# Split fp32r products for two small sums, and another order of the output matrix's making, in a fused linear-attention and state-space kernel

## The chip, the cores and the metric

The kernel runs on one core of one Trainium2 chip. A core has a matrix engine (PE, whose weight loads are listed apart as PEld), a vector engine (DVE), a scalar engine (ACT), a general engine (POOL) and a queue engine (SP) that issues most transfers; each works through its own instructions in order. The metric is the time of one execution on the device in microseconds (us), lower is better.

## The reference

From one input x (2048 positions, 448 channels) two branches are computed and mixed by a gate for each position:

```python
g = sigmoid((x * gate_w).sum(-1, keepdims=True))
# branch a: linear attention without a mask, 16 heads of 28 channels
q, k, v = split(x @ wqkv)
phi = lambda t: where(t > 0, t + 1, exp(t)) + 1e-6
pq, pk = phi(q), phi(k)
kv  = einsum("bhsd,bhse->bhde", pk, v)
z   = pk summed over positions
num = einsum("bhqd,bhde->bhqe", pq, kv)
den = einsum("bhqd,bhd->bhq", pq, z) + 1e-6
a = (num / den) @ wo
# branch b: a state-space convolution of x along the positions, plus x * D_skip
b = irfft(rfft(x) * rfft(K))[:S] + x * D_skip
out = g * a + (1 - g) * b
```

K is the convolution's kernel, made from a table of decay rates. For the tables in use K is nearly constant over all 2048 positions, so that the convolution is a running sum of x times one number for each channel; the kernel counts for how many channels this holds, and only if that is not all 448 a general convolution is run at the end. With these inputs it is not run.

## The kernel before, in words

The 2048 positions are 16 chunks of 128. Matrix products that need more than the engine's fast format gives are split: a number is written as a high part in fp32r and the low rest, and high·high, low·high and high·low are added up (11 products for a chunk with 448 inner channels). `low` makes such a rest, `ACT.copy` into an fp32r tile makes the high part.

**Main loop** (c = 0 to 13, then a closing part for c = 14 and 15). For each chunk PE projects k of chunk c+1 and q of chunk c (`project`, `pieces`, L319), adds pk·x into four running 128x448 sums (`do_g`, L388) and makes the running sum of x inside the chunk (`do_v`, L395 and L396). ACT and DVE make pk and pq (`k_feature`, `k_high`, `k_low`, `q_post`); `k_low` also adds pk into `zb`, so that at the end `zb` summed over its 128 partitions is z. `v_post` multiplies the running sum by its taps, sends its last row to row c of the tile `u` through SP (L402), and POOL adds it to the chunk's output (`v_add`, L407).

**Closing part** (from `c = NC - 2`). In program order: k of chunk 15 and its features; the last `v_post`; q of chunk 14; one block of `do_g(14)`; an fp32 product of a ones column with `oks` (the count of channels, L626) and an fp32 product of a 128x128 ones matrix with `zb` (L627), which leaves z on all partitions; `q_post(14)`; ACT copies z back to `zb` (L629); POOL starts the products pq·z (`norm_a`, L517); the rest of `do_g(14)`; the gate of chunk 14 (`gate`, L372 to L374); a PE transposition of the gates (`gates_b`, L564), which needs that gate; the denominators of chunks 0 and 1 (`norm_b`, `norm_d`, `norm_c`); and the four blocks of `do_g(15)`, each copied out by ACT (L646). `okn` receives the count (L637).

**Making the output matrix.** `inter` multiplies a 0/1 matrix `gcat` with `u` in fp32 (L660): the carry of each chunk from all chunks before it. Then K·V of each head pair (`kv_products`, L691, 32 fp32 instructions), its masking and splitting (`kv_split`, `kv_low`), and its product with wo for four groups of heads (`m_products`, L671; `m_high`, L675; `m_low`, L679). Group 3 is laid out anew: four small transfers (L725 three, L726 one) move rows of it below the rows of the other groups. Between these PE transposes chunk 0 (`turn_pe`) and finishes q of chunk 15 (`q_run`).

**Last loop** (c = 0 to 15). In each step DVE takes chunk c-1 out of PSUM and SP writes it (`final_b`, L607); `norm_c(c+2)` scales pq by 1/den with two POOL instructions (L540, L546) and one DVE instruction (L543); PE transposes chunk c+1 (L577), and ACT and DVE split the result into high and low (`turn_split`, L584, L585); ACT adds the carry's gate rows (`tail`, L588); POOL starts pq·z of chunk c+6 (`norm_a`); PE makes 11 products for chunk c (`attend`, L602); DVE sums pq·z of chunk c+5 over the heads (`norm_b`, L522); every second step `norm_d` makes 1/den for two chunks (L527, L529).

The order on each engine is the order of the program text (a manual schedule). Tiles rotate in pools of named tags, so that an instruction can also wait for a buffer; `norm_a(c)` and `norm_b(c-2)` share one in this way.

Of the kernel before, what the change touches and what calls it, by code (L numbers as in the profile page):

```python
# [7 lines left out]
F32 = mybir.dt.float32  # L8
# [7 lines left out]
P = 128  # L16
# [23 lines left out]
FAR = 2.0 ** 100  # L40
GIN = 9 + NC
L1, L0 = 32, 64
PAD = S + P
MAGIC = 1.5 * 2.0 ** 23
TWO_PI = 6.283185307179586
# [85 lines left out]
def gated_mix_kernel(ctx: ExitStack, tc: tile.TileContext, xin, wq_d, wv_d, wo_d, abc_d, ldt_d, dsk_d,  # L131
# [23 lines left out]
    tri = const.tile([P, P], F32R, name="tri")  # L155
    ident = const.tile([P, P], F32, name="ident")
    mask = const.tile([DJ, DJ], F32, name="mask")
    gcat = const.tile([NC - 1, RX], F32, name="gcat")
    sel = const.tile([P, 1], F32, name="sel")
    ones = const.tile([P, P], F32, name="ones")  # L160
    rows = const.tile([P, S], F32, name="rows")
    near, dsk = (rows[:, i * D:(i + 1) * D] for i in range(2))
    u = const.tile([NC, D], F32, name="u")
    zb = const.tile([P, D], F32, name="zb")
    kv = const.tile([DJ, J, DJ], F32, name="kv")
    ldt = const.tile([DJ, J], F32, name="ldt")
    sm = const.tile([DJ, 16, J], F32, name="sm")
    oks = const.tile([DJ, 1], F32, name="oks")
    trir = const.tile([P, P], F32, name="trir")

    xp = work.enter_context(tc.tile_pool(name="xp", bufs=4))
# [6 lines left out]
    DVE.memset(warm, 1.0)  # L178
    POOL.memset(zb, 0.0)
    POOL.memset(rows[DT:RX, 2 * D:], 0.0)  # L180

    xt, xn, turned, plain = {}, {}, {}, {}

# [187 lines left out]
    def gate(a, b):  # L371
        DVE.tensor_scalar(out=e1[:, a:b], in0=e1[:, a:b], scalar1=1.0, scalar2=None, op0=ALU.add)  # L372
        DVE.reciprocal(out=og[:, a:b], in_=e1[:, a:b])
        DVE.tensor_scalar(out=og[:, a:b], in0=og[:, a:b], scalar1=-1.0, scalar2=1.0, op0=ALU.mult, op1=ALU.add)  # L374
# [5 lines left out]
    def do_g(c, blocks=range(4)):  # L380
        w = xn[c]
        for i in blocks:
            a = w[:, 64 + i * P:64 + (i + 1) * P]
            b = w[:, XC - NAT + 64 + i * P:][:, :P] if i < 3 else None
            seq = [(a, pkh[c]), (a, pkl[c]), (b, pkh[c])] if i < 3 else \
                  [(a, pkh[c]), (a[:, :64], pkl[c])][::1 if c == 0 else -1]
            for n, (a, b) in enumerate(seq):
                PE.matmul(g[i][:a.shape[1], :D], lhsT=a, rhs=b, start=c == 0 and n == 0,  # L388
                          stop=c == NC - 1 and n == len(seq) - 1)
# [3 lines left out]
    def do_v(c):  # L393
        v = vt[c] = ps.tile([P, 512], F32, name="v", tag="v%d" % (c % 2))
        PE.matmul(v[:, :D], lhsT=tri, rhs=xn[c][:, :D], start=True, stop=False)  # L395
        PE.matmul(v[:, :D], lhsT=tri, rhs=xn[c][:, XC - NAT:], start=False, stop=True)  # L396

    def v_post(c):
        t = tp.tile([P, D], F32, name="t", tag="v0")
        DVE.tensor_tensor(out=t, in0=vt.pop(c)[:, :D], in1=near, op=ALU.mult)  # L400
        if c < NC - 1:
            SP.dma_start(out=u[c:c + 1], in_=t[P - 1:P])  # L402
            v_add(c, t)
        return t

# [43 lines left out]
    q_post(0, qo)  # L449
    split_n(2)  # L450
    qo = project(1, wqh, wql, D + 2, "v0")
    DVE.memset(ones, 1.0)
    q_post(1, qo)
    steps(1)
    skip(0)
# [2 lines left out]
    for c in range(2, NC - 2):  # L458
        if c + 3 < NC:
            load_x(c + 3)  # L460
        if c == 2:
            for o, i in ((mask, mask_d), (gcat, gcat_d), (sel, sel_d)):
                SP.dma_start(out=o, in_=i)
        if c == 4:
            SP.dma_start(out=wv, in_=wv_d)
            SP.dma_start(out=wo, in_=wo_d)
        vs = VS.get(c, ())
        ko = project(c + 1, wkh, wkl, D, "v1" if c in (2, 4) else "k")
        for v in vs[:1]:
            do_v(v)  # L470
        split_t(c + 2)
        k_feature(c + 1, ko)
        k_high(c + 1)
        if c > 5:
            for v in vs[:1]:
                v_post(v)
        k_low(c + 1)
        qo = project(c, wqh, wql, D + 2, "q")
        if c == 5:
            steps(1)  # L480
        else:
            for v in vs[1:]:
                do_v(v)
        q_post(c, qo)
        if c == 5:
            v_post(0)
        else:
            for v in vs[1:]:
                v_post(v)
        if c < 5:  # L490
            steps(2 if c == 4 else 1)
        if c == 3:
            DVE.tensor_copy(tri, trir)
        do_g(c)
        if c == 5:
            do_v(1)
        if c < 4:
            skip(c - 1)
        split_n(c + 2)
        if c == 5:  # L500
            v_post(1)
        for j in {11: (0, 1), 12: (2, 3)}.get(c, ()):
            w = xn_p.tile([P, NX], F32R, name="wo", tag="n")[:DJ, :2 * D].rearrange("p (i d) -> p i d", i=2)
            woh.append(w[:, 0])
            wol.append(w[:, 1])
            ACT.copy(woh[j], wo[:, j])
            low(POOL, wol[j], wo[:, j], woh[j])
# [84 lines left out]
    def attend(c, cuts):  # L592
        av[c] = []
        h, l = th.pop(c), tl.pop(c)
        for i, (lo, hi) in enumerate(cuts):
            pool, tag = ((p3, "a"), (p3, "a"), (ps, "v0"), (ps, "k"))[(c + i) % 4]
            a = pool.tile([P, 512], F32, name="a", tag=tag)
            av[c].append((a, lo, hi))
            seq = [(u_[:, j], w_[:, j]) for u_, w_ in ((h, mh), (l, mh), (h, ml)) for j in (2, 0, 1)]
            seq[6:6] = [(h[:, 3], mh[:, 3]), (l[:RX, 3], rc[0][:RX])]  # L600
            for n, (u_, w_) in enumerate(seq):
                PE.matmul(a[:, lo:hi], lhsT=u_, rhs=w_[:, lo:hi], start=n == 0, stop=n == 10)  # L602

# [9 lines left out]
            ACT.copy(pq[:, c, lo:hi], a[:, lo:hi])  # L613

    c = NC - 2
    gate(0, c)
    ko = project(c + 1, wkh, wkl, D, "k")
    do_v(c + 1)
    k_feature(c + 1, ko)
    k_high(c + 1)  # L620
    k_low(c + 1)
    vl = v_post(c + 1)
    qo = project(c, wqh, wql, D + 2, "q")
    do_g(c, (0,))
    zo = ps.tile([P, 512], F32, name="zo", tag="v0")
    PE.matmul(zo[:1, D:D + 1], lhsT=ones[:DJ, :1], rhs=oks, start=True, stop=True)  # L626
    PE.matmul(zo[:, :D], lhsT=ones, rhs=zb, start=True, stop=True)  # L627
    q_post(c, qo)
    ACT.copy(zb, zo[:, :D])  # L629
    norm_a(0)  # L630
    norm_a(1)
    do_g(c, (1, 2, 3))
    gate(c, c + 1)
    g2 = gates_a(1, NC - 1)
    POOL.memset(rows[DT:RX, :2 * D], 0.0)
    last = gates_b(g2, "pkl")
    DVE.tensor_copy(okn, zo[:1, D:D + 1])  # L637
    norm_bd(0)
    norm_c(0)
    last()  # L640
    norm_a(2)
    norm_bd(1)
    norm_c(1)
    for i in range(4):
        do_g(c + 1, (i,))
        ACT.copy(gs[i], g[i][:, :D])  # L646
# [8 lines left out]
    def inter():  # L655
        o = ps.tile([P, 512], F32, name="z", tag="v0")
        r = tp.tile([P, D], F32R, name="rc", tag="w")
        z = tp.tile([P, D], F32R, name="zs", tag="v0")
        rc.append(r)
        PE.matmul(o[:RX, :D], lhsT=gcat, rhs=u[:NC - 1], start=True, stop=True)  # L660
        ACT.copy(z[DT:RX], o[DT:RX, :D])
        DVE.scalar_tensor_tensor(out=r[DT:RX], in0=z[DT:RX].bitcast(F32), scalar=sel[DT:RX],
                                 in1=o[DT:RX, :D], op0=ALU.mult, op1=ALU.add)
# [30 lines left out]
    def kv_split(r, kvp):  # L694
        m = 3 if r else 2
        DVE.tensor_tensor(out=kv[:, 2 * r:m],
                          in0=kvp[:DJ, 2 * r * DJ:m * DJ].rearrange("p (j d) -> p j d", d=DJ),
                          in1=mask[:, None, :].to_broadcast([DJ, m - 2 * r, DJ]), op=ALU.mult)
        if r:
            a, b = (w.rearrange("p (h d) -> p h d", h=4) for w in (kvp[:DJ, 3 * DJ:4 * DJ], mask))  # L700
            DVE.tensor_tensor(out=kv[:, 3, :DT].rearrange("p (h d) -> p h d", h=4), in0=a[:, :, DS:], in1=b[:, :, DS:],
                              op=ALU.mult)
            a, b = (w[:, :, :DS].rearrange("p h (j d) -> p h j d", j=3) for w in (a, b))
            DVE.tensor_tensor(out=kv[:, 3, DT:].rearrange("p (j h d) -> p h j d", j=3, h=4), in0=a, in1=b, op=ALU.mult)
        rs = slice(2 * r, 2 * r + 2)
        ACT.copy(kvh[:, rs], kv[:, rs])

# [6 lines left out]
    k1 = kv_products(1)  # L714
    k0 = kv_products(0)
    kv_split(1, k1)
    norm_a(3)
    kv_low(1)
    kv_split(0, k0)
    kv_low(0)  # L720
    mrows(3, ps, "k")
    norm_bd(2)
    mrows(2, ps, "v0")
    for j, eng in ((2, SP), (0, ACT), (1, SP)):
        eng.dma_start(out=wk2[DJ:, :, j].bitcast(F32), in_=shl[DT + 16 * j:DT + 16 * j + 16].bitcast(F32))  # L725
    SP.dma_start(out=mh[DT:, 3].bitcast(F32), in_=shl[:DT, 1].bitcast(F32))  # L726
    o0 = turn_pe(0)
    norm_c(2)
    norm_a(4)
    mrows(0, p3, "a")  # L730
# [74 lines left out]
def _layout(inputs):  # L805
# [36 lines left out]
    s = np.arange(P)  # L842
    lag = s[None, :] - s[:, None]
    k = np.arange(NC)[None, :] - np.arange(NC)[:, None]
    gcat = np.zeros((NC - 1, RX))
    gcat[:, DT:] = np.repeat(k[:-1] > 0, 3, axis=1)
    sel = np.zeros((P, 1))
    sel[DT:RX, 0] = -1.0 * (np.arange(RX - DT) % 3 == 1)
    h = np.arange(DJ) // DH
# [34 lines left out]
```

## Time and profile before

| | us |
|---|---|
| median of 3 runs | 179.49 |
| lowest, highest | 179.27, 180.06 |
| the profiled execution's own time | 179.93 |
| its span in the trace | 178.1 |
| PE busy in it | 172.5 |
| POOL busy in it | 119.5 |
| DVE busy in it | 115.9 |
| ACT busy in it | 94.7 |

What lies around the span (179.93 less 178.1, 1.8 us) is start and end of the execution and carries no instruction. In a row of the trace's timeline the first number is the start in us from the span's beginning, the second the time up to the end of the last instruction merged into the row; then come the engine, the line of the kernel, the operation, what it writes and reads with partitions x elements, how many were merged, and in brackets how long its engine sat idle before it and what ended that. In the chain of waits a row is a piece of the path that ended last: start, length, engine and line.

### The profile page before, as it was taken

Reading aid. Unit: us, or ns where it says so; the run is one execution under the profiler, and the core shown is the slowest. Engines: PE = TensorE matmul, PEld = TensorE weight load, DVE = VectorE, ACT = ScalarE, POOL = GpSimd, SP = SyncE. Lnnn points to the kernel's source line nnn. Section 1 sums busy time; section 2 is a strip of 40 time slices with the busy share of each in tenths; the row PEclk is TensorE's granted clock in tenths of the full one; section 3 lists DMA queues with packets and bytes.
Section 4 is the critical chain, followed back from the end, with each engine's and each line's share of the span. In section 5 each row is a group of like instructions: output and inputs, shape, how many; then the busy total and the mean of one; then the engine's idle time right before and its main releaser. Section 6 shows DMA issues by size and latency. Waiting matters only on the chain.

```text
span 178.1 us, 2750 instructions
## 1 busy us (share of the span) xinstructions
PE 172.5 (97%) x879; PEld 152.0 (85%) x879; DVE 115.9 (65%) x238; ACT 94.7 (53%) x212; POOL 119.5 (67%) x124
## 2 busy tenths in 40 slices
PE   6999999999999999999999999999999999999991
PEld 2598999999999999999989999877879999899990
DVE  1747647688857173562824519389799999998551
ACT  3779388884537244372536653444565455564441
POOL 3167577879259969687598999059289998773100
PEclk9999999999999999999999999999999999999999
DMA  5999974198003303033033000000031221131222
GB/s 166 416 291 271 249 203 153 10 375 239 4 1 118 118 0 120 5 118 101 18 118 122 0 0 0 0 4 5 6 60 68 88 98 62 67 119 73 109 76 82
DMA packets 7784, 18.40 MB, mean 103 GB/s; under 512 B 1755, under 2 KB 4520, under 8 KB 7768
## 3 DMA queue, kind: packets, MB, share of 16 engines
q1 hardware_dynamic: 7720, 18.16, 32.2%
q8 instruction: 7, 0.11, 0.3%
q10 hardware_dynamic: 48, 0.06, 0.2%
q14 instruction: 9, 0.07, 0.1%
HBM read 14.20 MB, written 3.67 MB: 100 GB/s over the span
## 4 chain that ended last, share of the span: by engine, by line
PE 91%; DVE 5%; issue 1%; ACT 1%; ACTq 0%
PE g L388 20%; PE q L319 19%; PE a L602 16%; PE k L319 15%; PE v L319 6%; PE tr L577 3%; PE q L246 3%; PE v L396 2%; PE v L395 2%; PE m L671 1%; DVE th L585 1%; DVE ot L607 1%; DVE den L527 1%; DVE den L522 1%; PE tr L691 1%
## 5 line engine op out<-in xcount | busy, mean ns | idle before, releaser
L602 PE MATMUL a<-wk,th 128*128 128x448 f32 (+1 forms) x170 | 39.5, 364 | 0.0
L388 PE MATMUL g<-pkh,xn 128*128 128x448 f32 x112 | 36.1, 370 | 0.0
L602 PEld LDWEIGHTS a<-wk,th 128*128 128x128 f32 x170 | 29.6, 189 | 2.6 <-DMA wk<-shl 0.3
L319 PE MATMUL k<-wk,xt 128*128 128x448 f32 x132 | 30.4, 376 | 0.0
L347 DVE SCALAR_TENSOR_TENSOR k<-k,e 128x448 f32<-128x448 f32 x12 | 7.6, 632 | 33.9 <-ACT e L346 33.9
L319 PE MATMUL q<-wqh,xt 128*128 128x450 f32 x120 | 27.7, 368 | 0.0
L319 PEld LDWEIGHTS k<-wk,xt 128*128 128x128 f32 x132 | 25.1, 190 | 2.9 <-ACT wk L416 0.8
L407 POOL TENSOR_TENSOR y<-y,t 128x448 f32<-128x448 f32 x16 | 18.6, 1163 | 13.4 <-DVE t L400 13.1
L224 POOL TENSOR_TENSOR xn<-xr,xn 128x448 fp32r<-128x448 f32 x16 | 19.2, 1200 | 8.7 <-ACT xn L234 8.4
L319 PEld LDWEIGHTS q<-wqh,xt 128*128 128x128 f32 x120 | 22.7, 189 | 2.7 <-issue 0.7
L517 POOL TENSOR_TENSOR prod<-pq,zb 128x448 f32<-128x448 f32 x16 | 18.6, 1162 | 8.3 <-ACT zb L629 6.0
L388 PE MATMUL g<-pkl,xn 128*128 128x448 f32 x64 | 23.5, 367 | 0.0
L388 PEld LDWEIGHTS g<-pkh,xn 128*128 128x128 f32 x112 | 21.1, 188 | 2.8 <-issue 0.2
L345 ACT ACTIVATE e<-k 128x448 f32<-128x448 f32 x12 | 6.5, 545 | 30.2 <-PE k L319 30.2
L240 POOL TENSOR_TENSOR y<-xr,rows 128x448 f32<-128x448 f32 x16 | 18.7, 1168 | 0.0
L224 POOL TENSOR_TENSOR xt<-xr,xt 128x512 fp32r<-128x512 f32 x14 | 18.3, 1306 | 0.2 <-ACT xt L228 0.2
L540 POOL TENSOR_TENSOR pn<-pq,den 128x336 f32<-128x336 f32 x16 | 12.1, 754 | 7.7 <-DVE den L529 5.6
L584 ACT CAST th<-tr 128x512 fp32r<-128x512 f32 x16 | 9.4, 589 | 9.2 <-PE tr L577 9.0
L607 DVE SCALAR_TENSOR_TENSOR ot<-y,og,a 128x448 f32<-128x448 f32 (+1 forms) x17 | 10.4, 615 | 4.6 <-PE a L602 4.6
L613 ACT COPY pq<-a 128x448 f32<-128x448 f32 (+1 forms) x17 | 8.8, 517 | 6.5 <-DVE ot L607 5.7
L388 PEld LDWEIGHTS g<-pkl,xn 128*128 128x128 f32 x64 | 11.2, 175 | 1.2 <-issue 0.2
L319 PE MATMUL q<-wql,xt 128*128 128x450 f32 x45 | 11.7, 364 | 0.0
(135 smaller groups left out, 305.0 us busy)
## 6 DMA issues: line engine op xcount, KB each, us to landing
xr<-in SPq DMA_DIRECT2D x15, 512.0 KB, 3.5
out<-ot SPq DMA_DIRECT2D x15, 224.0 KB, 1.9
pq<-in SPq DMA_DIRECT2D x4, 448.0 KB, 13.3
y<-in SPq DMA_DIRECT2D x2, 480.0 KB
y<-in SPq DMA_DIRECT2D x2, 450.0 KB, 7.4
wv<-in SPq DMA_DIRECT2D x1, 896.0 KB, 5.5
wo<-in SPq DMA_DIRECT2D x1, 784.0 KB
y<-in SPq DMA_DIRECT2D x1, 448.0 KB
```

Of the source, the lines that this page charges most:

```text
L224: eng.tensor_tensor(out=o, in0=r, in1=h.bitcast(F32), op=ALU.subtract)
L240: POOL.tensor_tensor(out=y[:, c], in0=plain[c][:, :D], in1=dsk, op=ALU.mult)
L319: PE.matmul(o[:, :n], lhsT=a, rhs=b, start=run.n == 1, stop=not seq)
L347: DVE.scalar_tensor_tensor(out=pks[c], in0=pks[c], scalar=1.0, in1=e, op0=ALU.add, op1=ALU.max)
L388: PE.matmul(g[i][:a.shape[1], :D], lhsT=a, rhs=b, start=c == 0 and n == 0, stop=c == NC - 1 and n == len(seq) - 1)
L407: POOL.tensor_tensor(out=y[:, c], in0=y[:, c], in1=t, op=ALU.add)
L517: POOL.tensor_tensor(out=pd[c], in0=pq[:, c], in1=zb, op=ALU.mult)
L540: POOL.tensor_tensor(out=n[:, :3, :DJ].rearrange("p j (h d) -> p j h d", h=4), in0=a, in1=r[:, :H - 4].rearrange("p (j h) -> p j h", j=3)[ ...
L584: ACT.copy(h, ov)
L602: PE.matmul(a[:, lo:hi], lhsT=u_, rhs=w_[:, lo:hi], start=n == 0, stop=n == 10)
L607: DVE.scalar_tensor_tensor(out=ot[:, lo:hi], in0=y[:, c, lo:hi], scalar=og[:, c:c + 1], in1=a[:, lo:hi], op0=ALU.mult, op1=ALU.add)
L613: ACT.copy(pq[:, c, lo:hi], a[:, lo:hi])
```

## The change

The sum of pk over partitions becomes two fp32r products (high and low part of `zb`), placed between and behind blocks of `do_g(14)`, which now all stand ahead of the gate. The carry product is one fp32r product over 47 partitions: `u` is written twice by SP, to rows 0 to 14 and 32 to 46; ACT rounds all of it into `uw`, and POOL replaces rows 32 to 46 by their low rest, while `gcat` holds the same 0/1 rows in both places. The count goes from a column to a row by an SP transfer at chunk 7 and is summed by DVE at chunk 9. The split of K·V, the four groups of the output matrix, the four transfers (all on SP now), the denominators of chunk 1 and two products of q of chunk 15 stand in another order, and `attend` takes its 11 products group by group, with the correction rows last.

```diff
+UL = 32
+UZ = UL + NC - 1
...
-    gcat = const.tile([NC - 1, RX], F32, name="gcat")
+    gcat = const.tile([UZ, RX], F32, name="gcat")
+    gcr = const.tile([UZ, RX], F32R, name="gcr")
...
-    ones = const.tile([P, P], F32, name="ones")
+    ones = const.tile([P, P], F32R, name="ones")
...
-    u = const.tile([NC, D], F32, name="u")
+    u = const.tile([UZ, D], F32, name="u")
...
+    okr = const.tile([1, DJ + 1], F32, name="okr")
...
+    POOL.memset(u, 0.0)
+    POOL.tensor_copy(ones, warm[:, :P])
...
-            SP.dma_start(out=u[c:c + 1], in_=t[P - 1:P])
+            for k in (c, UL + c):
+                SP.dma_start(out=u[k:k + 1], in_=t[P - 1:P])
...
-    DVE.memset(ones, 1.0)
...
+            DVE.tensor_copy(gcr, gcat)
+        if c == 7:
+            SP.dma_start(out=okr[:, None, :DJ], in_=oks[:, None, :])
+        if c == 9:
+            DVE.tensor_reduce(out=okr[:, DJ:], in_=okr[:, :DJ], op=ALU.add, axis=AX.X)
+            DVE.tensor_copy(okn, okr[:, DJ:])
...
-            seq = [(u_[:, j], w_[:, j]) for u_, w_ in ((h, mh), (l, mh), (h, ml)) for j in (2, 0, 1)]
-            seq[6:6] = [(h[:, 3], mh[:, 3]), (l[:RX, 3], rc[0][:RX])]
+            seq = [(u_[:, j], w_[:, j]) for j in (2, 0, 1) for u_, w_ in ((h, mh), (l, mh), (h, ml))]
+            seq += [(h[:, 3], mh[:, 3]), (l[:RX, 3], rc[0][:RX])]
...
     c = NC - 2
+    POOL.memset(rows[DT:RX, D:2 * D], 0.0)
     gate(0, c)
     ko = project(c + 1, wkh, wkl, D, "k")
     do_v(c + 1)
+    uw = xt_p.tile([P, 2 * NAT], F32R, name="uw", tag="t")[:UZ, :D]
     k_feature(c + 1, ko)
+    ACT.copy(uw, u)
+    low(POOL, uw[UL:], u[UL:], uw[UL:])
     k_high(c + 1)
     k_low(c + 1)
+    zh, zl = (tp.tile([P, D], F32R, name=n, tag=t) for n, t in (("zh", "w"), ("zl", "pk")))
+    qo = project(c, wqh, wql, D + 2, "q")
+    do_g(c, (0, 1, 2))
+    zo = ps.tile([P, 512], F32, name="zo", tag="v0")
+    ACT.copy(zh, zb)
+    low(DVE, zl, zb, zh)
+    PE.matmul(zo[:, :D], lhsT=ones, rhs=zh, start=True, stop=False)
+    do_g(c, (3,))
+    PE.matmul(zo[:, :D], lhsT=ones, rhs=zl, start=False, stop=True)
     vl = v_post(c + 1)
-    qo = project(c, wqh, wql, D + 2, "q")
-    do_g(c, (0,))
-    zo = ps.tile([P, 512], F32, name="zo", tag="v0")
-    PE.matmul(zo[:1, D:D + 1], lhsT=ones[:DJ, :1], rhs=oks, start=True, stop=True)
-    PE.matmul(zo[:, :D], lhsT=ones, rhs=zb, start=True, stop=True)
     q_post(c, qo)
     ACT.copy(zb, zo[:, :D])
     norm_a(0)
     norm_a(1)
-    do_g(c, (1, 2, 3))
     gate(c, c + 1)
     g2 = gates_a(1, NC - 1)
-    POOL.memset(rows[DT:RX, :2 * D], 0.0)
+    POOL.memset(rows[DT:RX, :D], 0.0)
     last = gates_b(g2, "pkl")
-    DVE.tensor_copy(okn, zo[:1, D:D + 1])
     norm_bd(0)
     norm_c(0)
     last()
     norm_a(2)
-    norm_bd(1)
-    norm_c(1)
+    norm_b(1)
...
-        PE.matmul(o[:RX, :D], lhsT=gcat, rhs=u[:NC - 1], start=True, stop=True)
+        PE.matmul(o[:RX, :D], lhsT=gcr, rhs=uw, start=True, stop=True)
...
+
+    def kv_high(r):
         rs = slice(2 * r, 2 * r + 2)
         ACT.copy(kvh[:, rs], kv[:, rs])
...
     kv_split(1, k1)
+    kv_high(1)
     norm_a(3)
     kv_low(1)
     kv_split(0, k0)
+    o3 = m_products(3, ps, "k")
+    o2 = m_products(2, ps, "v0")
+    m_high(3, o3)
+    kv_high(0)
+    m_low(3, o3)
     kv_low(0)
-    mrows(3, ps, "k")
+    m_high(2, o2)
+    for j in (2, 0, 1):
+        SP.dma_start(out=wk2[DJ:, :, j].bitcast(F32), in_=shl[DT + 16 * j:DT + 16 * j + 16].bitcast(F32))
+    SP.dma_start(out=mh[DT:, 3].bitcast(F32), in_=shl[:DT, 1].bitcast(F32))
+    norm_d(1, 1)
+    norm_c(1)
+    m_low(2, o2)
+    o0 = turn_pe(0)
+    q_run(2)
     norm_bd(2)
-    mrows(2, ps, "v0")
-    for j, eng in ((2, SP), (0, ACT), (1, SP)):
-        eng.dma_start(out=wk2[DJ:, :, j].bitcast(F32), in_=shl[DT + 16 * j:DT + 16 * j + 16].bitcast(F32))
-    SP.dma_start(out=mh[DT:, 3].bitcast(F32), in_=shl[:DT, 1].bitcast(F32))
-    o0 = turn_pe(0)
     norm_c(2)
     norm_a(4)
     mrows(0, p3, "a")
...
-    gcat = np.zeros((NC - 1, RX))
-    gcat[:, DT:] = np.repeat(k[:-1] > 0, 3, axis=1)
+    gcat = np.zeros((UZ, RX))
+    for r in (0, UL):
+        gcat[r:r + NC - 1, DT:] = np.repeat(k[:-1] > 0, 3, axis=1)
```

## The prediction

> **What bounds the kernel now.** I read the page first: its sums, its strips of 40 slices, and the idle time that the groups list.
>
> ```profile
> span 178.1 us, 2750 instructions
> ...
> PE 172.5 (97%) x879; PEld 152.0 (85%) x879; DVE 115.9 (65%) x238; ACT 94.7 (53%) x212; POOL 119.5 (67%) x124
> ...
> DVE  1747647688857173562824519389799999998551
> ...
> PE 91%; DVE 5%; issue 1%; ACT 1%; ACTq 0%
> ...
> L347 DVE SCALAR_TENSOR_TENSOR k<-k,e 128x448 f32<-128x448 f32 x12 | 7.6, 632 | 33.9 <-ACT e L346 33.9
> ```
>
> PE is busy 97% of the span, so work taken from PE is worth its length, as long as the others keep up. In the main loop they do: DVE idles 33.9 us before one group alone. But slices 30 to 36 of DVE's strip (129 to 160 us) are all 9: in the last loop DVE is full too. There its average of 65% says nothing.
>
> Then the chain of waits through the part that changes. Pieces of PE follow each other almost without a gap:
>
> ```profile
> 115.96 0.12 PE zo L626 x2
> 116.08 0.95 PE zo L627 x2
> 117.03 1.61 PE g L388 x8
> 118.64 0.11 PE o L564
> ...
> 120.97 0.93 PE z L660 x2
> 121.89 0.40 PE q L319
> 122.30 1.57 PE k L691 x16
> ```
>
> A split product takes 1.61 / 8 = 0.20 us here; an fp32 product of the same width takes 0.95 or 0.93.
>
> **The change part by part.** *PE's own time.* Removed: the count's 0.12 and the sum's 0.95; added: two products, 0.40. That is -0.67. The carry goes from 0.93 to 0.20: -0.73. Together -1.40 us, if nobody is late.
>
> *The gate is late.* All of `do_g(14)` now stands ahead of the transposition of the gates (L564), with the two short products in it. PE reaches the transposition at 118.64 - 0.67 = 117.97. What it waits for is on DVE; the timeline of the same place:
>
> ```profile
> 115.22 0.63 DVE L357 SCALAR_TENSOR_TENSOR zb<-k,zb 128x448 f32<-128x448 f32 x1 [0.61 <-ACT pkh L351]
> 115.77 0.61 DVE L357 SCALAR_TENSOR_TENSOR pkl<-k,pkh 128x448 fp32r<-128x448 f32 x1
> 116.30 0.61 DVE L400 TENSOR_TENSOR t<-v,rows 128x448 f32<-128x448 f32 x1
> ...
> 117.68 2.26 POOL L517 TENSOR_TENSOR prod<-pq,zb 128x448 f32<-128x448 f32 x2 [5.96 <-ACT zb L629]
> ...
> 118.44 0.09 PEld L564 LDWEIGHTS o<-ident,og 128*14 128x14 f32 x1 [0.17 <-DVE okn L637]
> ...
> L252 ACT CAST wk<-y 128x448 fp32r<-128x448 f32 x3 | 1.6, 565 | 0.7 <-DMA y<-in 0.7
> ...
> L224 DVE TENSOR_TENSOR wk<-y,wk 128x448 fp32r<-128x448 f32 x3 | 1.7, 621 | 0.0
> ```
>
> Today DVE's chain just meets PE's: the weight load at 118.44 waited 0.17. The change adds to exactly this chain. `zb` is there at 115.22 + 0.63 = 115.85. ACT rounds it, 0.57 by the cast of the same shape, until 116.43. DVE, done with pkl at 116.38, then makes `zl`, 0.62 by the subtraction of the same shape, until 117.07. Only then comes L400, which started at 116.30; each DVE instruction starts some 0.07 before the last one's listed end (115.22 + 0.63 against 115.77), so it starts at 117.0, 0.7 later. From its start to the weight load lie 118.44 - 116.30 = 2.14 today, a little less without the `okn` copy. So the load comes at about 119.1. PE stands still for 119.1 - 118.0 = 1.1 us, and everything behind the transposition is 0.6 later than before, not 0.67 earlier. Bounds: -0.67 if the gate could be ready, +0.7 if DVE's whole delay counts; I take +0.6. Behind PE stand `do_g(15)` and K·V. ACT's rounding also holds up its exponentials for q of chunk 14, but these are done before DVE needs them.
>
> *The carry.* The -0.73 counts after that: K·V starts at 122.30 + 0.6 - 0.73 = 122.17, 0.13 earlier. Its next condition is the copies of the four sums:
>
> ```profile
> 119.44 2.19 ACT L646 COPY gs<-g 128x448 f32<-128x448 f32 x4 [0.29 <-PE g L388]
> ```
>
> They end at 121.63, now 122.23; the fourth pair of products, first to need the last copy, stands 3 x 0.2 behind the start, at 122.8. No wait, 0.5 to spare. `uw` is long done: ACT makes it in the 0.63 that DVE needs for L347, POOL its low rows at 114 to 116, within the 5.96 that it idles before 117.68.
>
> *The output matrix.* Rows of that stage:
>
> ```profile
> 125.69 0.37 PE L671 MATMUL m<-wo,kvl 112*112 112x448 f32 x1
> ...
> 126.31 0.53 ACT L675 CAST shl<-m 112x448 fp32r<-112x448 f32 x1
> 126.32 0.39 DVE L224 TENSOR_TENSOR kvl<-kv,kvh 112x224 fp32r<-112x224 f32 x1 [0.45 <-ACT kvh L706]
> ...
> 126.87 0.62 DVE L679 TENSOR_TENSOR shl<-m,shl 112x448 fp32r<-112x448 f32 x1 [0.16 <-ACT shl L675]
> ...
> 128.06 0.17 DVE L527 SCALAR_TENSOR_TENSOR den<-den,e 128x16 f32<-128x16 f32 x1
> 128.27 0.25 DVE L529 RECIPROCAL den<-den 128x16 f32<-128x16 f32 x1
> ...
> 128.92 0.59 DVE L543 TENSOR_TENSOR pn<-pq,den 128x48 f32<-128x48 f32 x1
> ...
> 129.96 0.68 DVE L585 TENSOR_TENSOR th<-tr,th 128x512 fp32r<-128x512 f32 x1
> ...
> 131.09 0.60 DVE L522 TENSOR_REDUCE den<-prod 128x16 f32<-128x448 f32 x1
> ...
> 131.44 0.91 PEld L602 LDWEIGHTS a<-wk,th 128*128 128x128 f32 x5 [0.34 <-DMA wk<-shl]
> ```
>
> Group 3's product ends at 125.69 + 0.37 = 126.06; its high copy began only at 126.31, behind another on ACT. The new order puts it first: 126.06 - 0.13 + 0.05 = 125.98, so DVE's low part starts at 126.5 instead of 126.87, 0.35 earlier. But DVE's list from there to the sum for chunk 3 (131.09) grows. Today it takes 131.09 - 126.87 = 4.22 without a gap. Added: kvl, which stood ahead, 0.39 less overlap, 0.32; L527, L529 and L543 of chunk 1, moved here from before the carry, 0.17 + 0.25 + 0.2 with their small gaps 0.65. Saved: L543 of chunk 2 (0.59) follows its own reciprocal and no longer a POOL instruction, some 0.25. The sum is 4.22 + 0.72 = 4.94, so the sum for chunk 3 starts at 126.5 + 4.94 = 131.45, 0.35 later than now.
>
> *The first products of the last loop.* Their wait of 0.34 for a transfer goes: that group's rows are now needed seventh instead of third. In its place the second product needs the low part of chunk 0 (L585), which the same DVE list moves from 130.64 to about 131.0; PE comes to it some 0.2 before. Gain here 0.1 to 0.2. All four transfers now follow each other on SP (0.8 each by the row below) from 127.1, land 3.2 after issue, the third at about 131.9, needed near 132.1: just in time, 0.2 late at worst.
>
> ```profile
> 127.53 1.62 SPq L725 DMA_DIRECT2D wk<-shl  x2
> ...
> wk<-shl SPq DMA_DIRECT2D x2, 56.0 KB, 3.2
> ```
>
> *Who is late next: POOL.*
>
> ```profile
> 131.77 1.16 POOL L517 TENSOR_TENSOR prod<-pq,zb 128x448 f32<-128x448 f32 x1 [0.86 <-DVE den L522]
> ...
> 135.11 0.76 POOL L540 TENSOR_TENSOR pn<-pq,den 128x336 f32<-128x336 f32 x1
> 135.82 0.40 POOL L546 TENSOR_TENSOR pn<-pq,den 128x128 f32<-128x128 f32 x1
> ...
> 136.08 0.60 PE L577 MATMUL tr<-ident,pn 128*128 128x128 f32 x4
> ```
>
> POOL's product for chunk 5 waits until DVE's sum for chunk 3 gives its buffer back. From 131.77 POOL runs without a gap (two further instructions of 1.16 between the first and the second row) to chunk 3's scaling, which ends at 136.22, and PE transposes chunk 3 from 136.08: POOL meets PE here with nothing to spare. DVE's 0.35 becomes 0.35 on PE. What PE had in hand at the first products is used up in waiting.
>
> *Does the loop take it back?*
>
> ```profile
> 142.78 0.69 DVE L585 TENSOR_TENSOR th<-tr,th 128x512 fp32r<-128x512 f32 x1 [0.30 <-ACT th L584]
> ...
> 150.06 1.07 DVE L527 SCALAR_TENSOR_TENSOR den<-den,e 128x32 f32<-128x32 f32 x1
> ...
> 152.62 0.63 PE L577 MATMUL tr<-ident,pn 128*128 128x128 f32 x4 [0.23 <-DVE pn L543]
> ```
>
> At 142.78 DVE waits for PE's chunk and starts afresh with it; from there the same instructions run in the same order to 152.62, so the 0.35 stays. After that PE sets the end.
>
> *Edits at nothing.* The second transfer of each row of `u`, the rounding of `gcat` and the count at chunks 7 and 9 lie in the main loop; SP waits there, and DVE's idle 33.9 us cover its three small instructions. Without cover these would be under 0.2 us each. POOL's clearing of rows, cut in two, comes before work that starts later anyway.
>
> **Sum.** Span 178.1 + 0.35 = 178.45, the profiled execution 179.93 + 0.35 = 180.3. The median of the runs is 0.44 below that execution, so the forecast is 179.9: no change, where 0.5% (0.9 us) is about what a measurement can tell.
>
> **Rivals.** *Faster: the gate is not late.* If ACT's and DVE's steps overlapped more than their rows say, PE's 1.40 would come through up to group 3's product, DVE's list would start 1.2 earlier, and chunk 3's transposition 0.8 earlier instead of 0.35 later: 179.5 - 0.85 = 178.6; with DVE and POOL out of the way too, 1.40 and the transfer's 0.34, 177.8. For it speaks PE's 97%; against it, that today's weight load already waits 0.17 for this chain.
>
> *Between: POOL's tie gives way.* Then -0.13, -0.34 and a little remain: 179.0, still no change.
>
> *Slower: one collision in the loop.* L527 took 0.17 at 128.06 and 1.07 at 150.06, where a POOL product was running; DVE's two-input instructions wait for POOL there. Shifted against POOL by a few tenths, one more of them between 142.78 and 152.62 can wait for a whole POOL instruction, 1.16 - 0.2, some 0.9. DVE is full there, and PE waits for L543 at 152.62, so that decides from the first 0.1 on: 179.9 + 0.9 = 180.8. The Trainium skill states such a lock (SBUF — State Buffer, section "Who interferes with whom"): a DVE instruction with two SBUF inputs and a GpSimd instruction that reads SBUF exclude each other, and whichever issues first holds the port for its whole instruction. The trace agrees (0.17 against 1.07). By that rule `zl`, with both inputs in SBUF, could wait too, but POOL, idle for 5.96 before 117.68 and with one short task more now, has nothing to run at 116.4.
>
> *The change doesn't do what it says:* the two sums stay at the fp32 price, and the wait for the gate stays too: 179.9 + 0.7 = 180.6. Against it: every split product in the trace takes 0.20.
>
> **How the numbers follow.** Forecast 0.46, gate not late 0.17, POOL's tie giving way 0.13, collision 0.22, fp32 price 0.02. The forecast's own range is 179.4 to 180.5; some 0.04 of it lies above 180.4, and 0.02 of the tie case below 178.6. Faster 0.19, no change 0.52, slower 0.29. The range for 8 in 10 goes down to the first price of the faster rival, 178.6, and up to 180.9.
>
> **What would show it.** Right: PE idle about 1.1 us before L564, ended by DVE's gate; the sum and the carry at 0.2 a product; DVE's sum for chunk 3 at 131.4 and chunk 3's transposition at 136.4, released by POOL. Wrong: L564 with no wait, or chunk 3's transposition earlier than 136.08; then I sized DVE's lists wrongly. If DVE and PE part only after 142.78, it is the collision.

## The result and the profile after

| | before | after |
|---|---|---|
| median of 12 runs, us | 179.50 | 179.67 |
| lowest, highest | 179.23, 180.06 | 179.15, 179.78 |
| profiled execution | 179.93 | 179.75 |
| its span | 178.1 | 178.0 |

The ratio after to before is 1.0001, with a 95% interval of 0.9991 to 1.0012. No change can be told; the forecast was 179.9, in a range of 178.6 to 180.9. The page of the kernel after (span, busy times, the strip of DVE, shares of the chain):

```profile
span 178.0 us, 2782 instructions
...
PE 170.5 (96%) x876; PEld 151.9 (85%) x876; DVE 117.7 (66%) x240; ACT 95.7 (54%) x214; POOL 121.5 (68%) x128
...
DVE  1747637898867384462733619376799999998551
...
PE 84%; DVE 9%; POOL 2%; issue 2%; ACT 1%; ACTq 0%; DVEq 0%
```

PE is busy 2.0 us less, and almost nothing of it reaches the end: PE's share of the chain of waits falls from 91% to 84%, DVE's rises from 5% to 9%, and POOL appears with 2%. The timeline of the kernel after, where the split sum and the gate stand:

```profile
114.63 0.62 DVE L363 SCALAR_TENSOR_TENSOR zb<-k,zb 128x448 f32<-128x448 f32 x1 [0.61 <-ACT pkh L357]
...
115.29 0.57 ACT L642 CAST zh<-zb 128x448 fp32r<-128x448 f32 x1 [0.69 <-DVE zb L363]
...
115.89 0.62 DVE L230 TENSOR_TENSOR zl<-zb,zh 128x448 fp32r<-128x448 f32 x1
...
116.44 0.62 DVE L406 TENSOR_TENSOR t<-v,rows 128x448 f32<-128x448 f32 x1
...
118.37 0.15 DVE L380 TENSOR_SCALAR og<-og 128x1 f32<-128x1 f32 x1
...
118.58 0.28 PE L576 MATMUL o<-ident,og 128*14 128x128 f32 x1 [1.17 <-DVE og L380]
```

This is the wait that was forecast: rounding on ACT, then `zl` on DVE, then the old list behind it; PE stands still for 1.17 us before the transposition of the gates. And later, up to chunk 3's transposition:

```profile
121.02 0.46 PE L677 MATMUL z<-uw,gcr 47*112 47x448 f32 x1
121.40 0.47 PE L325 MATMUL q<-wqh,xt 128*128 128x450 f32 x1
121.72 1.54 PE L708 MATMUL k<-gs,wv 128*112 128x112 f32 x14
...
123.49 0.27 DVE L713 TENSOR_TENSOR kv<-k,mask 112x112 f32<-112x112 f32 x1 [0.47 <-PE k L708]
...
130.83 1.70 PEld L614 LDWEIGHTS a<-wk,th 128*128 128x128 f32 x9 [0.40 <-DVE th L597]
...
131.23 0.61 DVE L534 TENSOR_REDUCE den<-prod 128x16 f32<-128x448 f32 x1
...
131.91 1.16 POOL L529 TENSOR_TENSOR prod<-pq,zb 128x448 f32<-128x448 f32 x1 [0.19 <-DVE den L534]
...
135.25 0.74 POOL L552 TENSOR_TENSOR pn<-pq,den 128x336 f32<-128x336 f32 x1
...
136.05 0.69 PE L589 MATMUL tr<-ident,pn 128*128 128x128 f32 x4 [0.27 <-POOL pn L552]
...
PE tr L589 <- DVE pn L555: 0.5, 1, 0.5
```

The chain runs as the forecast had it: DVE's sum for chunk 3, POOL's products, chunk 3's scaling on POOL, and PE waiting for it (0.27). The last row is from the sums of waits: in the last loop PE waits once more, 0.5, for DVE's scaling, at chunk 9 (0.23 before). The products that the change made, in the chain of waits (`zo` the two halves of the sum, `z` the carry):

```profile
116.59 0.21 PE zo L644
...
117.21 0.22 PE zo L646
...
121.09 0.39 PE z L677
```

The halves of the sum cost what was forecast, 0.2 each; the carry costs almost twice that.

To compare two executions, I cut each trace at the starts of the same PE rows, and took differences, since the first loads alone let the first block of 22 projection products start anywhere from 8.7 to 9.7 us after the span's beginning. "q14" is q of chunk 14, "gates" the transposition of the gates, "K·V" its first product, "tr3" and "tr9" the transpositions of chunks 3 and 9, "end" the end of the last product.

| stage, us | before | after | difference |
|---|---|---|---|
| first block to q14 | 103.59 | 102.93 | -0.66 |
| q14 to gates | 5.53 | 6.23 | +0.70 |
| gates to K·V | 3.67 | 3.14 | -0.53 |
| K·V to tr3 | 13.94 | 14.33 | +0.39 |
| tr3 to tr9 | 16.54 | 16.70 | +0.16 |
| tr9 to end | 21.60 | 21.34 | -0.26 |
| sum | 164.87 | 164.67 | -0.20 |

The four middle rows are the change's schedule, +0.72 in all. The first and the last, -0.92 together, are in stages that the change hardly touches; the forecast had nothing for them. The chain of waits of the kernel before and then of the kernel after, rows of start, length, line and number of products:

```profile
50.93 2.24 PE k L319 x11
...
53.57 2.25 PE q L319 x11
...
155.95 2.25 PE a L602 x11
```

```profile
50.80 2.21 PE k L325 x11
...
53.42 2.25 PE q L325 x11
...
156.02 2.22 PE a L614 x11
```

The same eleven k products take 2.21 instead of 2.24, and the last loop's 2.22 instead of 2.25; q's, of the chunk shown, take 2.25 in both.

### The profile page after: what moved, and what is told of

It reads as the page before. It is cut to its first block, busy times and chain, and to the rows that moved or that the text cites. A ratio compares the mean times of both kernels' runs of the same rounds, so it can differ in the third digit from the quotient of the medians.

```text
span 178.0 us, 2782 instructions
## 1 busy us (share of the span) xinstructions
PE 170.5 (96%) x876; PEld 151.9 (85%) x876; DVE 117.7 (66%) x240; ACT 95.7 (54%) x214; POOL 121.5 (68%) x128
## 3 DMA queue, kind: packets, MB, share of 16 engines
HBM read 14.22 MB, written 3.67 MB: 101 GB/s over the span
## 4 chain that ended last, share of the span: by engine, by line
PE 84%; DVE 9%; POOL 2%; issue 2%; ACT 1%; ACTq 0%; DVEq 0%
PE g L394 20%; PE q L325 18%; PE k L325 15%; PE a L614 13%; PE v L325 6%; PE q L252 3%; PE tr L589 3%; PE v L402 2%; PE v L401 2%; DVE den L534 1%; DVE th L597 1%; DVE pn L555 1%; DVE den L539 1%; POOL prod L529 1%; DVE wk L696 1%
## 5 line engine op out<-in xcount | busy, mean ns | idle before, releaser
L614 PE MATMUL a<-wk,th 128*128 128x448 f32 (+1 forms) x170 | 36.6, 360 | 0.1
L230 POOL TENSOR_TENSOR xn<-xr,xn 128x448 fp32r<-128x448 f32 x16 | 18.6, 1165 | 9.9 <-ACT xn L240 8.6
L246 POOL TENSOR_TENSOR y<-xr,rows 128x448 f32<-128x448 f32 x16 | 19.4, 1210 | 0.0
```

What stands on the lines that cost most here:

```text
L230: eng.tensor_tensor(out=o, in0=r, in1=h.bitcast(F32), op=ALU.subtract)
L246: POOL.tensor_tensor(out=y[:, c], in0=plain[c][:, :D], in1=dsk, op=ALU.mult)
```

## The experiments

All twelve were timed in five rounds beside the kernel before. An interval is the 95% interval of the ratio to it.

**Is the pace a matter of the execution?** The kernel before, unchanged.

> The kernel before, unchanged: how much two traces of one kernel differ. Until chunk 14's q, where the two kernels' PE work is the same, the changed kernel's trace is 0.59 us ahead (112.35 against 112.94), because 11 products take 2.21 in it and 2.24 to 2.27 in the trace of before. If the pace belongs to the execution, this trace may show 2.21 too, and chunk 14's q may begin anywhere from 112.3 to 113.0. If it belongs to the kernel (where its tiles lie), it is 2.24 to 2.27 again and q begins at 112.9. Time 179.5 by both.

179.43, ratio 0.9995 (0.9983 to 1.0008). Cut as above, its stages are 103.52, 5.54, 3.66, 13.96, 16.49 and 21.57, each within 0.07 of the first trace. So the stages are good to about 0.1, and the same kernel shows the same pace again.

**The sum alone.** Before, with the sum of k split and the count by a transfer:

```diff
+    ACT.copy(zh, zb)
+    low(DVE, zl, zb, zh)
+    PE.matmul(zo[:, :D], lhsT=ones, rhs=zh, start=True, stop=False)
...
+    PE.matmul(zo[:, :D], lhsT=ones, rhs=zl, start=False, stop=True)
...
-    PE.matmul(zo[:1, D:D + 1], lhsT=ones[:DJ, :1], rhs=oks, start=True, stop=True)
-    PE.matmul(zo[:, :D], lhsT=ones, rhs=zb, start=True, stop=True)
```

> The kernel before with only the sum of k as two fp32r products in the changed kernel's place and the count by a transfer; carry and order as before. Theory: PE waits 1.1 for the gate before the transposition, which comes 0.6 to 0.7 later, and the rest follows: 180.1. Rival (the sum's saving of 0.67 is had, or the loop hides both): 178.8 to 179.5.

180.42, ratio 1.0047 (1.0033 to 1.0061): slower. Its timeline at the gate:

```profile
118.26 0.28 PE L570 MATMUL o<-ident,og 128*14 128x128 f32 x1 [1.17 <-DVE og L376]
```

The same 1.17, and q14 to gates is 6.23, as in the whole change. The price of the late gate thus belongs to the sum. But not all of the 0.9 in the time is schedule. Cut as above, the four middle stages cost 1.05, and the first and the last give 0.45 back (PE's pace again, see below): all stages add up to 165.47, 0.60 more than before. Behind ACT's last instruction the span goes on for 3.40 us, against 2.97 in the kernel before. The trace's records of SP show why: in every one of the fourteen executions of this document SP pauses for 0.40 to 0.41 us in that stretch, always behind its 155th recorded instruction. In the kernel before, with 158 such instructions, this falls after SP has told the other engines to finish (POOL goes on 2.24 behind ACT's last instruction). With one transfer more it falls just ahead of that, and POOL goes on at 2.67. In the kernel after, with 175, it falls at 0.18, where SP waits for the last output anyway. What makes SP pause there is not shown.

**The carry alone.** Before, with the doubled rows of `u` and the fp32r product:

```diff
-        PE.matmul(o[:RX, :D], lhsT=gcat, rhs=u[:NC - 1], start=True, stop=True)
+        PE.matmul(o[:RX, :D], lhsT=gcr, rhs=uw, start=True, stop=True)
```

> The kernel before with only the carry as one fp32r product over 47 partitions; sum of k, count and order as before. Theory (the gains are real and each later wait takes one away): PE gains 0.73 after the gate, and nothing is added to DVE's lists, so group 3's low part, DVE's sum for chunk 3 and chunk 3's transposition all come 0.7 earlier: 178.8. Rival (the last loop is full on DVE and POOL, and its end does not depend on when it starts): 179.3 to 179.6.

179.88, ratio 1.0021 (1.0011 to 1.0030). My theory fell, and the time lies above the rival's too: gates to K·V became 0.54 shorter, and K·V to tr3 0.45 longer. Its timeline:

```profile
121.46 1.73 PE L700 MATMUL k<-gs,wv 128*112 128x112 f32 x16
...
121.89 1.13 POOL L523 TENSOR_TENSOR prod<-pq,zb 128x448 f32<-128x448 f32 x1
121.93 1.16 DVE L549 TENSOR_TENSOR pn<-pq,den 128x48 f32<-128x48 f32 x1
...
123.11 0.69 DVE L671 SCALAR_TENSOR_TENSOR rc<-zs,sel,z 48x448 fp32r<-48x448 f32 x1
...
123.81 0.27 DVE L705 TENSOR_TENSOR kv<-k,mask 112x112 f32<-112x112 f32 x1
```

K·V's first half is through at 121.46 + 1.73 = 123.19, but DVE masks it only at 123.81. Chunk 1's scaling, a DVE instruction with two SBUF inputs, took 1.16 beside a POOL product that had started 0.04 earlier. The timeline of the kernel before, chunk 0's scaling, chunk 1's and the masking:

```profile
120.30 0.21 DVE L543 TENSOR_TENSOR pn<-pq,den 128x48 f32<-128x48 f32 x1
...
122.03 1.17 DVE L543 TENSOR_TENSOR pn<-pq,den 128x48 f32<-128x48 f32 x1
...
123.91 0.28 DVE L696 TENSOR_TENSOR kv<-k,mask 112x112 f32<-112x112 f32 x1
```

The first of them, chunk 0's, took 0.21, with only a clearing (a write) running on POOL, from 120.00 to 120.84. This is the lock that the Trainium skill describes (SBUF — State Buffer, section "Who interferes with whom"); the numbers agree. The kernel before pays it as well, but there K·V's first half ends at 122.30 + 1.57 = 123.87, as late as DVE's list, so it costs nothing. In the kernel after, chunk 1's scaling stands elsewhere, and the masking begins at 123.49 as soon as PE is done (its row waited 0.47 for PE). Whether moving the denominator is what brings the carry's gain through is tried below, and it is not. Here 3.49 us stand behind ACT's last instruction: SP has 173 instructions, its pause falls at 1.34, behind the wait for the last output, and POOL goes on at 2.77 instead of 2.24. The stages themselves add up to 164.80, 0.07 less than before, so the +0.37 in the time is that stretch and not the carry.

**The gate early.** After, with chunk 14's gate ahead of `v_post` and of q's feature, its transposition in another PSUM bank:

```diff
+    ACT.activation(e1[:, c:c + 1], qo[:, D:D + 1], AF.Exp, scale=-1.0)
+    gate(c, c + 1)
     vl = v_post(c + 1)
-    q_post(c, qo)
+    feature(pq[:, c], qo)
...
-    gate(c, c + 1)
...
-    last = gates_b(g2, "pkl")
+    last = gates_b(g2, "pkl", "k")
```

> The changed kernel with chunk 14's gate made on DVE ahead of the last v_post and of q's feature, and the gates transposed into another PSUM bank, so that the transposition waits for neither. Theory: PE's wait of 1.17 before the transposition falls under 0.2, K*V starts 1.0 earlier, chunk 3's transposition comes about 1.0 earlier (135.1 where it was 136.05), and the time is 178.7. Rival (the loop sets the end): the wait is gone, but the time is 179.3 to 179.7.

178.84, ratio 0.9967 (0.9955 to 0.9979). q14 to gates falls from 6.23 to 4.89: PE no longer waits. Gates to K·V rises from 3.14 to 3.98, because K·V's bank now comes free late (rows below, with the best kernel). Of the 1.34 us, 0.50 are left after these two stages, and the later ones keep them (16.67 from tr3 to tr9 against 16.70).

**Where PE's pace comes from.** The change adds tiles among the constants (`gcr`, `okr`, and larger `gcat` and `u`), and everything allocated behind them moves. By the addresses that the tiles get, the four tiles that hold transposed x (PE loads them for k and q; in the last loop transposed pq) begin 96 bytes behind a multiple of 256 in each partition in the kernel before, and at a multiple in the kernel after. Four kernels with unused bytes among the constants or between the pools, otherwise unchanged, and then one that moves these four tiles alone:

```diff
     trir = const.tile([P, P], F32, name="trir")
+    pad = const.tile([P, 8], F32, name="pad")
```

> The kernel before with one unused tile of 32 bytes a partition, which moves every tile behind the constants by 32 bytes. In the four programs so far 11 products of k take 2.21, 2.23, 2.245 and 2.26 where these tiles start 0, 64, 96 and 32 bytes behind a multiple of 128 in SBUF; before has 96, the changed kernel 0, and the shift gives 0. Theory (the pace comes from the place): k takes 2.21 and the last loop's products 2.21 instead of 2.25, q stays at 2.25, chunk 14's q begins 0.6 earlier, and with 0.04 on seven steps after the last wait the time is 178.6. Rival (the pace comes from the order of the work or from chance): 179.5, k at 2.245.

```diff
     trir = const.tile([P, P], F32, name="trir")
+    pad = const.tile([P, 24], F32, name="pad")
```

> The changed kernel with one unused tile of 96 bytes a partition, so that its tiles lie as far behind a multiple of 128 as in the kernel before. Theory (the place gives the changed kernel 0.85 us that its other parts lose again): k and the last loop's products at 2.245, and the time is 180.5, 0.9 over before: the price of the schedule alone. Rival (the pace has another cause): 179.6.

```diff
     trir = const.tile([P, P], F32, name="trir")
+    pad = const.tile([P, 40], F32, name="pad")
```

> The kernel before with 160 unused bytes, so that the moved tiles start at a multiple of 256 as in the changed kernel (a shift of 32 put them 128 behind one, and k took 2.225). Theory (256 counts): 11 products of k take 2.21, the last loop's 2.21 to 2.22, time 178.7. Rival (128 counts, the rest is something else in the changed kernel): k 2.225, time 178.9.

```diff
     xt_p = work.enter_context(tc.tile_pool(name="xt", bufs=4))
+    gap = work.enter_context(tc.tile_pool(name="gap", bufs=1)).tile([P, 40], F32, name="gap")
     xn_p = work.enter_context(tc.tile_pool(name="xn", bufs=7))
```

> The kernel before with 160 unused bytes between the tiles xt and xn, so that xt (the loaded operand of k, q and, as th, of the last loop) stays 96 behind a multiple of 256, while xn, pkh and pkl (the operands of the sums pk*x) move to one. Theory (the loaded operand's place sets the pace): k stays at 2.245, the last loop at 2.25, the sums go from 2.242 to 2.23, time 179.3. Rival (the tiles behind xt, which the other engines read and write, set it): k 2.21, time 178.7.

```diff
+    gap = work.enter_context(tc.tile_pool(name="gap", bufs=1)).tile([P, 40], F32, name="gap")
     xt_p = work.enter_context(tc.tile_pool(name="xt", bufs=4))
+    gap2 = work.enter_context(tc.tile_pool(name="gap2", bufs=1)).tile([P, 24], F32, name="gap2")
     xn_p = work.enter_context(tc.tile_pool(name="xn", bufs=7))
```

> The kernel before with 160 bytes left free between the tiles of x and the four tiles of the tag that holds transposed x (and, in the last loop, the high and low parts of transposed pq), and 96 bytes behind these. So only these four tiles move, from 96 bytes behind a multiple of 256 to a multiple of 256; all other tiles keep their place against 256. Theory (PE's pace hangs on the place of the operand that PE loads): k at 2.21 per 11 products instead of 2.245, q of 450 columns unchanged at 2.25, time 178.7 (0.994 to 0.996), as with everything moved by 160 bytes. Rival (the place of the tiles of x, or of several together, decides): k stays at 2.245 and the time at 179.5 (0.999 to 1.001).

The third column is the mean over the chain's rows.

| kernel | bytes behind a multiple of 256 | 11 products of k | time, us | ratio and interval |
|---|---|---|---|---|
| before | 96 | 2.245 | 179.50 | |
| before, 32 bytes added | 128 | 2.225 | 178.93 | 0.9968 (0.9956 to 0.9980) |
| before, 160 bytes added | 0 | 2.21 | 178.68 | 0.9941 (0.9926 to 0.9957) |
| before, 160 bytes behind these tiles only | 96 | 2.245 | 179.83 | 1.0006 (0.9992 to 1.0020) |
| before, these tiles alone moved by 160 | 0 | 2.21 | 178.82 | 0.9960 (0.9945 to 0.9975) |
| after | 0 | 2.21 | 179.67 | 1.0001 (0.9991 to 1.0012) |
| after, 96 bytes added | 96 | 2.245 | 180.24 | 1.0041 (1.0027 to 1.0055) |

Rows of the chain of waits, of the kernel with 160 bytes added, of the one with these bytes behind the four tiles only, and of the one where the four tiles alone move:

```profile
50.30 2.21 PE k L320 x11
```

```profile
50.54 2.24 PE k L320 x11
```

```profile
50.17 2.21 PE k L321 x11
...
52.79 2.26 PE q L321 x11
```

The first shift was expected to give the whole gain, with 128 as the step that counts; it gave 2.225 and not 2.21, and 160 bytes gave the rest. The pace of k follows these four tiles alone, and the time follows the pace. The granted clock is no rival: it was 0.995 in the faster execution with the four tiles moved and 0.999 in the kernel before. One expectation fell: the sums pk·x, whose own operands moved in the kernel with bytes behind the four tiles, were to go from 2.242 to 2.23 for 11 products, and took 2.238; with the four tiles alone moved they took 2.227, and why is open. Once the four tiles are where the kernel before has them, the change costs +0.75 (180.24 against 179.49 alongside; 180.5 was expected). The sum of stages gives +0.65: +0.01, +0.69, -0.54, +0.40, +0.16 and -0.07.

**Chunk 1's denominator in its old place.** After, with the three DVE instructions of chunk 1 back before the carry:

```diff
-    norm_b(1)
+    norm_bd(1)
+    norm_c(1)
...
-    norm_d(1, 1)
-    norm_c(1)
```

> The changed kernel with chunk 1's denominator and scaling back where they were, ahead of the carry's rounding on DVE. Theory (both places cost alike): DVE then comes to K*V's mask 0.4 late, as in the run with the carry alone, but its later list is 0.65 shorter; chunk 3's transposition 0.2 to 0.3 earlier and the time 179.3 to 179.5. Rival (the move costs what I priced, 0.65, with nothing back): 179.0.

179.42, ratio 1.0004 (0.9976 to 1.0033); two of its twelve runs took 181.06 and 181.51, hence the wide interval. K·V to tr3 is 14.23, against 14.33, and gates to K·V 3.13, against 3.14: both places cost alike. Where the instructions stand late, DVE has them in its full list; where they stand early, chunk 1's scaling collides with POOL (1.10 from 122.02, a POOL product from 121.93) and the masking begins only at 123.84. Since neither stage is longer for it, the carry's gain in this kernel does not hang on the moved denominator; which other part of the new order keeps it was not tried.

**Best version.** After, with the gate early, and POOL's last addition (chunk 15) moved from before the last loop into its step 11:

```diff
-    v_add(c + 1, vl)
     tail(0)
...
+        if c == 11:
+            v_add(NC - 1, vl)
```

> The changed kernel with the early gate and with POOL's last addition of v (1.15 us, needed only by chunk 15) moved from ahead of the last loop to its step 11. Theory (POOL's tie): chunk 3's transposition no longer waits for POOL's scaling, which comes 1.1 earlier, and starts at 134.4 to 134.6 instead of 134.85; but DVE's wait at chunk 9 takes most of that back: 178.5 to 178.8. Rival (POOL sets the loop's end): 177.8.

178.08, ratio 0.9916 (0.9898 to 0.9934): faster than both kernels, and between the two expected times. tr3 to tr9 falls to 16.16 and PE no longer waits at chunk 9. Its timeline from the gate to K·V:

```profile
116.94 0.27 PE L576 MATMUL o<-ident,og 128*14 128x128 f32 x1
...
120.54 0.27 DVE L580 TENSOR_TENSOR phs<-o,phs 14x128 fp32r<-14x128 f32 x1
...
120.92 1.80 PE L709 MATMUL k<-gs,wv 128*112 128x112 f32 x16 [0.64 <-ACT zs L679]
```

The transposition of the gates has no wait. K·V still has one of 0.64; the view names ACT's `zs`, but DVE's `phs`, which reads the bank that K·V writes, ends later, at 120.81.

**That wait taken away too.** As the last, with the reading of the gates' bank ahead of chunk 0's denominator:

```diff
+    last()
     norm_bd(0)
     norm_c(0)
-    last()
```

> The run with early gate and late addition, in which K*V still waited 0.64 us before its first product: its PSUM bank is the one that the gates' transposition now uses, freed by a small DVE subtraction (L580) that stands behind chunk 0's denominator. Here that subtraction stands ahead of the denominator. Theory: the wait goes, K*V starts 7.9 to 8.1 after the start of chunk 14's q instead of 8.9, chunk 3's transposition follows DVE's list and comes 0.5 to 0.7 earlier: 177.5. Rival (DVE's fullness from chunk 3 to chunk 9 takes it back): 178.0.

178.14, ratio 0.9909 (0.9891 to 0.9926): no gain, where 177.5 was expected. Gates to K·V falls from 3.98 to 3.17, and K·V to tr3 rises from 14.24 to 14.91. Its timeline:

```profile
123.18 2.23 POOL L529 TENSOR_TENSOR prod<-pq,zb 128x448 f32<-128x448 f32 x2
...
124.30 1.36 DVE L230 TENSOR_TENSOR kvl<-kv,kvh 112x224 fp32r<-112x224 f32 x1 [0.45 <-ACT kvh L726]
```

`kvl`, with two SBUF inputs, took 1.36, against 0.39 in the kernel before: it starts 0.02 behind the second of the two POOL products and ends 0.24 behind that one's end. So the time is the rival's, but by this collision and not by DVE's fullness from chunk 3 on: tr3 to tr9 stays at 16.16. The profiled execution of this kernel (179.62) was the slowest of its seven: first block to q14 took 104.55, with a wait of 1.2 for DVE at 46.26. That stage lies ahead of this one.

## Why the forecast held, and which step failed

**The gate: right.** Forecast: PE still for 1.1 us, the rest 0.6 later. Measured: 1.17, and +0.70. The sum alone shows it, the early gate takes it away.

**The carry: right in kind, too large.** Forecast -0.73; gates to K·V became 0.53 shorter. The chain of waits counted the z product at 0.93 in the kernel before and 0.39 in the kernel after: z and the q product behind it start 0.38 apart instead of the 0.20 that I took for one split product.

**The output matrix: right in its path, and late.** Forecast: DVE's sum for chunk 3 at 131.45, 0.35 later than before, and chunk 3's transposition at 136.4, released by POOL. Measured: 131.23 and 136.05, released by POOL, in a trace that stands 0.59 ahead when q14 starts (102.93 + 9.42 against 103.59 + 9.35). Without this head start that is 131.82 and 136.64, 0.73 and 0.56 later than before, where 0.35 was forecast for both. DVE's list was sized well: from group 3's low part (126.24) to that sum it took 4.99, forecast 4.94. It began late, because K·V did: 0.30 behind the forecast, 0.10 from the gate and 0.20 from the carry. POOL passed on less than all of it: it met PE with some 0.17 in hand, not with nothing to spare. At the first products of the last loop the wait for a transfer went, as forecast, but PE's loads waited 0.40 for chunk 0's low part in its place.

**The loop: nearly.** I took the 0.35 to stay as it was. It grew by 0.16, a longer wait for DVE's scaling at chunk 9 (0.5 against 0.23). The rival of a whole collision there (0.9) didn't come. (The two rows that its price came from have 16 and 32 columns; the 32-column form took 0.27 at 133.82 in the kernel before, so the price is nearer 0.8.) Moving POOL's last addition took the wait away: tr3 to tr9 is 16.67 with the early gate alone and 16.16 with both.

**What failed: "edits at nothing" and the base of the sum.** The schedule costs 0.75 (180.24 against 179.49), not 0.35, by the sum of the small errors above. That the time did not rise comes from a term that the sum lacked: new tiles among the constants moved the tiles that PE loads from, and PE's 11 products became some 0.035 faster for each chunk's k and for each chunk of the last loop. In the trace the first and last stages give -0.92, in the medians it is 180.24 - 179.67 = 0.57; the gap between the two is not explained. The right net number thus has two errors of opposite sign in it, and that they nearly cancel is luck. Had the layout not moved, the time would have been 180.24, inside the range: slower by 0.4%, which the interval (1.0027 to 1.0055) tells from nothing, but within the 0.5% that the forecast called no change.

**The rivals.** "Gate not late" is refuted by the wait of 1.17, "the fp32 price" by the rows of 0.21 and 0.22, "POOL's tie gives way" by PE's wait of 0.27 for POOL's scaling. The early gate gave 178.84, near that rival's 178.6, but with the gain of the layout in it.

**Open.** What makes SP pause behind its 155th instruction. In the kernel with everything moved by 160 bytes, the last loop's 11 products take 2.24 instead of the 2.21 to 2.23 of after and of the kernel with the four tiles alone moved; which operand does that was not tried.

## What to carry to other kernels

A wait that PE's shorter work opens is best looked for on the list of the engine that feeds it: here 0.95 us of product became two short products and 1.17 us of standing still, because the split put two more steps ahead of an unrelated small instruction. Put small late instructions with many waiting behind them (a gate) ahead of long ones with none. Before crediting an edit with a gain, compare the pace of PE in stages that the edit doesn't touch: if it differs, the layout has moved, and unused bytes that put the layout back show the price of the edit itself. Compare the stretch behind the last instruction too: a few transfers more or fewer on SP changed it by up to 0.52 here.

## What the runs showed of the hardware that was not expected

**The place of the operand that PE loads sets the pace.** Eleven products of k (128x128 loaded, 448 columns) took 2.21 us with the loaded tile at a multiple of 256 bytes, 2.225 at 128 behind it, 2.245 at 96 behind. The sum alone has it at 64 and took 2.23, the carry alone at 32 and took 2.26. The same tiles loaded for q, with 450 columns, stay at a mean of 2.25 to 2.26 in all seven kernels of the table; why q has no gain is open. On the whole kernel the place is worth 0.75 us (179.57 to 178.82 with only these tiles moved).

**A lock between DVE and POOL can undo an earlier start.** A DVE instruction of 0.39 took 1.36 in the last kernel because it had come early enough to meet a POOL product: of the 0.81 gained from gates to K·V, the next stage lost 0.67. Chunk 1's scaling met one in the kernel before too (1.17); there it cost nothing, because PE was no earlier.

**SP pauses once at the end, and where it pauses decides what it costs.** In all fourteen executions it stands for 0.40 to 0.41 behind its 155th recorded instruction. The stretch behind ACT's last instruction is 2.94 to 3.04 where this is hidden, and 3.40 and 3.49 in the two kernels whose number of SP instructions puts it where the other engines wait for SP.
